# A gated sum of a recurrent attention and a feed forward part: the feed forward part goes ahead of the attention

## The chip, the cores and the metric

The kernel runs on one core of one Trainium2 chip. The time is that of the device in microseconds, the median of three runs; the profile is of one further execution. TensorE is PE, VectorE DVE, ScalarE ACT, GpSimd POOL and SyncE SP.

## What is computed

For an input x of 2048 rows and 1024 columns the output is g * a + (1 - g) * b. Here g is one number per row, b is a feed forward part with 3584 inner columns, and a is an attention that goes through 64 segments of 32 rows one after another: the first 8 of the 40 rows that a segment works on are the memory, which is the output of the segment before.

```python
        for s in range(n_seg):
            xs = x[:, s * seg_len:(s + 1) * seg_len, :].copy()
            h = jnp.concatenate([mem, xs], axis=1)
            q = jnp.einsum('btd,dhe->bhte', h, Wq)
            k = jnp.einsum('btd,dhe->bhte', h, Wk)
            v = jnp.einsum('btd,dhe->bhte', h, Wv)
            scores = jnp.einsum('bhqe,bhke->bhqk', q, k) * scale
            scores = jnp.where(mask[None, None], scores, -1000000000.0)
            p = _softmax(scores, axis=-1)
            o = jnp.einsum('bhqk,bhke->bhqe', p, v)
            o = jnp.einsum('bhte,hed->btd', o, Wo)
            mem = o[:, :M, :].copy()
            outs.append(o[:, M:, :])
...
    def _B_ref(x, w_gate, w_up, w_down):
        return _gelu(x @ w_gate) * (x @ w_up) @ w_down
    x = A_x
    g = _sigmoid((x * gate_w).sum(-1, keepdims=True))
    a = _A_ref(x, A_mem0, A_Wq, A_Wk, A_Wv, A_Wo, A_seg_len)
    b = _B_ref(x, B_w_gate, B_w_up, B_w_down)
    return g * a + (1 - g) * b
```

There are 32 heads of 128. Everything is bf16; a and b do not depend on each other.

## The kernel before

**How an operation gets its place.** There is no scheduler. `op(eng, fn, rd, wr, lane)` appends an operation to its engine's list in the order in which the program calls it, and derives its waits from the regions that it reads and writes. A DMA has a lane, and waits for the one before it in its lane. Each engine runs its list in order: a DMA on SP that waits holds up all DMAs behind it on SP.

**The weights of the attention.** Wq, Wk, Wv and Wo are 8 MB each, cut into 64 pieces of 512 KB (matrix m, half of the heads u, number i). On the chip there is room for 50 (lines 336 to 355, slots of 4 KB a partition): 36 pieces have a slot of their own, and 14 slots are shared by the two halves of a piece (`PAIRS`, line 311). Odd and even segments go through the halves in the opposite order, so each shared slot is loaded anew once a segment. Neighbouring shared slots are loaded as a group (`load_group`, line 422). A load reads the input, or a scratch in DRAM in which the group lies together, if the piece has been copied there: `keep` (line 389) writes a piece from its slot to scratch. Lines 937 and 939 call it, one or two pieces a segment, from segment 1 to segment 20, 28 pieces in all.

**The start.** Sixteen tiles of x (128 rows) are loaded to `px`, transposed on PE, copied by ACT and DVE, and written to `xq_scr` and `xr_scr` (`do_x`, line 504). POOL multiplies a tile by the gate's weights into the one buffer `gp` (line 527) and DVE sums it (line 529); `gate` (line 580) makes g out of the sums. The memory is transposed (line 494), and DVE copies it into the first segment's `hT0` (line 566) behind the DMA of line 533 that loads the rest of hT0. All 50 slots are filled in the order in which segment 0 uses them. The x tiles lie in the slots of Wo until these are loaded.

**A segment.** `proj` (line 771) projects 32 rows, 8 of memory and 24 of x (line 782 for q, k and v, lines 798 and 815 for Wo; four matmuls side by side on the columns of PE). The other 8 rows of x of each segment do not feed the memory, so their projections are made for four segments at once (`fill`, line 844, matmuls of line 852), stored to `qk_scr` and `v_scr` by POOL, and loaded back when due (`load_qk`, `load_v`). In segment 0 the fills of its own group and one of the next stand in front (`fill0`). `fold` (line 823) adds the two halves of the output in DVE, line 826 first; POOL stores them to `a_scr` (line 1012). `plan` (line 903) hangs these steps at fixed places of the walk over the weights.

**After the attention.** Line 1035 projects the outputs of the 8 other rows by Wo, for 16 segments at a time (256 matmuls), and ACT stores them to `a_scr`. Then comes the feed forward part, in four blocks `fb` of 512 rows. A block has 28 units (line 1085): 8 matmuls with w_gate and 8 with w_up make 128 inner columns; ACT and DVE make gelu and product in two and three operations. All of w_gate and w_up stays on the chip. The down projection (line 1139) goes over the block's rows in two halves; w_down comes by 1 MB through three buffers `wd` (`load_wd`), 14 loads a block. In the last block it lies whole in `wdF` (line 1120). `mix` (line 1055) takes a, which `load_a` (line 643) has loaded, and makes the output out of PSUM by two DVE operations. The gate and up weights are loaded from line 659 and lines 1047 to 1049.

Of the kernel before, what the change touches and what calls it, by code (L numbers as in the profile page):

```python
# [5 lines left out]
BF16 = mybir.dt.bfloat16  # L6
FP32 = mybir.dt.float32
# [203 lines left out]
def bass_gated_mix__memory_aug_recurrent_mem_tr__geglu_ffn__prompt_kernel(  # L211
# [34 lines left out]
    with ExitStack() as es:  # L246
# [16 lines left out]
        a_scr = nc.dram_tensor("a_scr", [NSEG, 4, SEG, 256], BF16)  # L263

# [71 lines left out]
        hosts = []  # L336
        for m in "kqvo":
            for i in range(8):
                if i in PAIRS[m]:
                    hosts.append([(m, 0, i), (m, 1, i)])  # L340
                else:
                    hosts += [[(m, 0, i)], [(m, 1, i)]]
# [46 lines left out]
        def keep(k, eng="sp"):  # L389
            t = slots[home[k]]  # L390
            op(eng, lambda e: e.dma_start(at_scr(k), t[:, :]), rd=[t.r()], wr=[("D", "w", k)], lane=f"keep{eng}")
            kept.add(k)
# [84 lines left out]
        cur[0] = slots[home["o", 0, 0]].off  # L477
        NPX = min(NT, 8)
        px = [al(f"px{i}", [128, D]) for i in range(NPX)]
        pm = al("pm", [128, D])  # L480
# [4 lines left out]
        hR1 = al("hR1", [128, KC, 32])  # L485
        dl = al("dl", [128, NT], FP32)
        assert cur[0] <= top
        memT = al("memT", [128, 64], at=oRc.off)

        mT = al("mT", [128, 16, NB])  # L490
        pw(mT, lambda e: e.memset(mT[0:NB, :, :], 0.0), True)
        pw(mT, lambda e: sel(e, mT[0:NB, :, :], ALU.is_ge, NEG, 0, [[0, 16], [1, NB]], -1))

        def tr_mem(e):
            e.transpose(PBV[5][:, 64:64 + NB], mT[0:NB, :, :].rearrange("p x i -> p (x i)"), ident[0:NB, 0:NB])
            for kc in range(KC):
                ins = e.transpose(PBV[5][:, kc * 8:(kc + 1) * 8], pm[0:8, kc * 128:(kc + 1) * 128], ident[0:8, 0:8])
            return ins
# [5 lines left out]
        def do_x(T):  # L504
            t = px[T % NPX]
            b = (XO, SS)[T % 2]
            x2 = T % 2

            def f(e):
# [8 lines left out]
            op("act", lambda e: e.activation(xq[x2][:, 0:2, :, :], pv[:, 0:2], ACTF.Copy), rd=[BK(b)], wr=[xq[x2].r(0, 512)])  # L518
            op("dve", lambda e: e.tensor_copy(xq[x2][:, 2:4, :, :], pv[:, 2:4]), rd=[BK(b)], wr=[xq[x2].r(512, 1024)])
            op("dve", lambda e: e.tensor_copy(to, PBV[b].rearrange("p (k i c) -> p k i c", k=KC, i=4)[:, :, :, NR:SEG]),  # L520
               rd=[BK(b)], wr=[to_r])
            op("act", lambda e: e.dma_start(xq_scr[T, :, :, :], xq[x2][:, :, :, :].rearrange("p i k c -> p i (k c)")),
               rd=[xq[x2].r()], wr=[("D", "xq", T)], lane=f"xw{x2}")
# [26 lines left out]
        op("sp", lambda e: e.dma_start(pm[0:8, :], mem0[:, :]), wr=[pm.r()], lane="pm")  # L550
# [4 lines left out]
        load_x(2)  # L555
        firsts = lambda m, r: [first(at_step(0, m, r, n)) for n in range(8)]
        for n in range(8):
            first(at_step(0, "k", 0, n))
            if n + 3 < NPX:
                load_x(n + 3)  # L560
        op("pe", tr_mem, rd=[pm.r(), mT.r(), ident.r()], wr=[BK(5)])
        op("dve", lambda e: e.tensor_copy(mS[:, 72:80], PBV[5][:, 64:64 + NB]), rd=[BK(5)], wr=[mS.r(72, 80)])
        op("dve", lambda e: e.tensor_copy(memT[:, :], PBV[5][:, 0:64]), rd=[BK(5)], wr=[memT.r()])
        do_x(0)
        load_h(0, "pool")
        op("dve", lambda e: e.tensor_copy(hT0[:, :, NR:32], memT[:, :].rearrange("p (k c) -> p k c", k=KC)),
           rd=[memT.r()], wr=[hT0.r()])
        for T in range(1, min(NT, 4)):
            do_x(T)
        for n in range(8):  # L570
            first(at_step(0, "q", 0, n))
            if n < 4:
                load_x(NPX + n)
        firsts("v", 0)

        def some_x(lo, hi):
            for T in range(lo, min(hi, NT)):
                do_x(T)

        def gate():  # L580
            op("act", lambda e: e.activation(gal[:, :], dl[:, :], ACTF.Exp, scale=-1.0), rd=[dl.r()], wr=[gal.r()])
            op("dve", lambda e: e.tensor_scalar(out=dl[:, :], in0=gal[:, :], scalar1=1.0, scalar2=None, op0=ALU.add),
               rd=[gal.r()], wr=[dl.r()])
            op("dve", lambda e: e.reciprocal(gal[:, :], dl[:, :]), rd=[dl.r()], wr=[gal.r()])


        cur[0] = res0
        FB = min(S, 512)
        NFB = S // FB
        TB = FB // 128  # L590
        NPS = (TB + 1) // 2
        xT = al("xT", [128, TB, 4, KC, SEG])
        WD = 4
        wd = [al(f"wd{i}", [128, WD, D]) for i in range(3)]
        CH = (2, 5, 7, 7, 7)
        assert sum(CH) == NJ
        jch = [(c, jj) for c, n in enumerate(CH) for jj in range(n)]
        wg, wu = [], []
        for c, n in enumerate(CH):
            wg.append(al(f"wg{c}", [128, KC, n * 128]))  # L600
            wu.append(al(f"wu{c}", [128, KC, n * 128]))
        GT = al("GT", [128, NJ, FB])
        assert cur[0] <= top
        free = [(low, res0), (cur[0], top)]

        def al2(name, shape, dt=BF16):
            nb = shape[1] * (4 if dt == FP32 else 2)
            for k, (lo, hi) in enumerate(free):
                if lo + nb <= hi:
                    free[k] = (lo + nb, hi)  # L610
                    return al(name, shape, dt, at=lo)
            raise AssertionError(name)
        asb = [al2(f"asb{t}", [128, D]) for t in range(4)]
        tp = [al2(f"tp{t}", [128, FB], FP32) for t in range(2)]
        s1 = al2("s1", [128, FB], FP32)
        dsb = [al2(f"dsb{t}", [128, 512], FP32) for t in range(2)]
        osb = [al2(f"osb{t}", [128, D]) for t in range(2)]

# [11 lines left out]
        NWD = NJ // WD  # L630
# [12 lines left out]
        def load_a(T):  # L643
            t = asb[T % 4]
            rd = [("D", "a", s) for s in range(4 * T, 4 * T + 4)] + [("D", "ar", T // 4, g) for g in range(4)]
            for n in range(4):
                op("sp", lambda e, n=n: e.dma_start(t[32 * n:32 * n + 32, :].rearrange("p (g c) -> p g c", g=4),
                                                     a_scr[4 * T + n].rearrange("g r c -> r g c")), rd=rd,
                   wr=[("asb", T % 4, n)] if n else [t.r()], lane=f"al{T % 4}{n}")

        oR = [al(f"oR{b}", [128, RB, 32], at=slots[home["q", 0, 2]].off + b * SB * 512) for b in range(NBK)]
        rbs = [al(f"rb{i}", [128, D], at=kT.off + 1536 - 2048 * i) for i in range(2)]
        assert a_bf.off == kT.off - 512 and rbs[0].off + 2048 <= res0
# [5 lines left out]
        early = [lambda b=b: load_oR(b) for b in range(NBK - 1)] + [lambda: load_xT(0), lambda: load_w(0), lambda: load_w(1)]  # L659


# [239 lines left out]
        STORE = [(m, i) for m in "vkq" for i in PAIRS[m]]  # L901

        def plan(s):
# [11 lines left out]
            if s == 0:  # L915
                on("k", 0, 0, lambda: some_x(4, 6))
                on("k", 0, 0, lambda: fill0("k", 0, B0, "k"))
                if NG > 1:
                    on("k", 0, 0, lambda: fill0("k", 0, B1, "o", 1, hR1))
                on("q", 0, 0, lambda: some_x(6, 8))  # L920
                on("q", 0, 0, lambda: [load_x(NPX + n) for n in range(4, 8)])
                on("q", 0, 0, lambda: (firsts("k", 1), firsts("q", 1)))
                on("q", 0, 0, lambda: fill0("q", 0, B1, "q"))
                on("v", 0, 0, lambda: some_x(8, 12))
                on("v", 0, 0, lambda: fill0("v", 0, B2, "o"))
                on("k", 0, 4, lambda: some_x(12, 16))
                on("k", 0, 4, lambda: [do_x(T) or load_x(T + NPX) for T in range(16, NT)])
                on("k", 0, 4, gate)
                on("k", 0, 5, lambda: firsts("v", 1))
                on("v", 0, 5, lambda: (firsts("o", 0), firsts("o", 1)))  # L930
# [4 lines left out]
            if 3 <= s < 3 + 2 * len(STORE):  # L935
                sm, si = STORE[(s - 3) // 2]
                on(*(("o", 1, 2) if sm == "v" else ("v", 1, 4)), lambda: keep((sm, ub, si), "act"))
            if 1 <= s <= 2 * len(PAIRS["o"]):
                on("k", 0, 4, lambda: keep(("o", s % 2, PAIRS["o"][(s - 1) // 2])))
# [86 lines left out]
        load_oR(NBK - 1)  # L1026
        for b in range(NBK):
            rb = rbs[b % 2]
            for hf in range(2):
# [9 lines left out]
                cp[("act", "dve")[hf]](rb[0:RB, hf * 512:hf * 512 + 512], PB[bk][0:RB, :], [BK(bk)], [rb.r(hf * 512, hf * 512 + 512)],  # L1039
                                       *([[ended]] if hf and b < 2 else []))  # L1040
                for g in (2 * hf, 2 * hf + 1):
                    op("act", lambda e, b=b, g=g, rb=rb: e.dma_start(a_scr[SB * b:SB * b + SB, g, NR:SEG, :], rb[0:RB, 256 * g:256 * g + 256]),
                       rd=[rb.r(256 * g, 256 * g + 256)] + [("D", "a", t) for t in range(SB * b, SB * b + SB)], wr=[("D", "ar", b, g)],
                       lane=f"sr{g}")


        load_w(2)
        load_w(3)
        load_w(4)
        for n in range(3):  # L1050
            load_wd()
# [132 lines left out]
```

## Time and profile before

| What | Value |
|---|---|
| median of 3 runs | 2289.18 us (2288.94 to 2291.22) |
| the profiled execution | 2283.55 us |
| its span, first to last instruction | 2281.7 us |
| mean granted TensorE clock | 0.982 |
| PE busy | 2054.7 us (90%) |
| DVE, ACT, POOL busy | 1044.2, 541.3, 423.7 us |
| moved by DMA | 647.47 MB, mean 284 GB/s |
| of it by queue q1 | 596.58 MB |

The busy time is an average over very different stages, so stages are read one by one. A row of the timeline is: start and length in us, engine, line, operation, what it writes and reads, how many, and in brackets the idle time before it and what ended it. The rows of DMA issues give size and the median time from issue to landing.

### The profile page before, as it was taken

The numbers are of one execution on the slowest core, as the hardware profiler recorded it, in microseconds if no ns is written. First come the engines' busy times: TensorE is split into PE (matmuls) and PEld (weight loads), VectorE is DVE, ScalarE is ACT, GpSimd is POOL, SyncE is SP. The second block draws the span as 40 slices with busy tenths as digits, with TensorE's granted clock in tenths as the row PEclk, the third lists the DMA queues.
The fourth block names the chain that finished last, engine by engine and source line by source line (L and its number), as shares of the span: only waits on it lengthen the run. The fifth ranks groups of instructions, "written<-read, shape, count | busy, mean of one in ns | idle before, by whom it ended". The sixth has DMA issues, their size and how long they took to land.

```text
span 2281.7 us, 69881 instructions
## 1 busy us (share of the span) xinstructions
PE 2054.7 (90%) x31393; PEld 979.5 (43%) x31393; DVE 1044.2 (46%) x2697; ACT 541.3 (24%) x1111; POOL 423.7 (19%) x819
## 2 busy tenths in 40 slices
PE   3498888989899999999999989998899999999999
PEld 2243444434444444444444444444454444444444
DVE  3344444444444545454554545454316346163462
ACT  1122222222222222222222222222113123031230
POOL 4422222222222222322222222221100000000000
PEclk9799999999999999999999999999999999999999
DMA  9999999989999999899999999899963530804420
GB/s 368 366 310 351 338 359 347 351 317 333 351 338 354 336 340 352 333 350 342 355 340 358 341 356 336 339 348 342 347 215 100 181 124 14 291 19 136 164 88 19
DMA packets 207002, 647.47 MB, mean 284 GB/s; under 512 B 21704, under 2 KB 90568, under 8 KB 174832
## 3 DMA queue, kind: packets, MB, share of 16 engines
q1 hardware_dynamic: 180288, 596.58, 71.8%
q0 software_dynamic: 13888, 26.31, 3.5%
q10 hardware_dynamic: 12528, 20.13, 2.4%
q8 instruction: 246, 4.03, 0.7%
q14 instruction: 52, 0.43, 0.1%
HBM read 596.85 MB, written 46.07 MB: 282 GB/s over the span
## 4 chain that ended last, share of the span: by engine, by line
PE 60%; DMA 29%; DVE 5%; ACT 2%; issue 2%; POOL 2%; SPq 0%; ACTq 0%; POOLq 0%; DVEq 0%
PE pb L782 20%; PE pb L1085 15%; DMA wall<-o_scr 10%; PE pb L1139 5%; PE pb L798 5%; DMA sl<-in_A_Wv_dram 3%; DMA o_scr<-oRc 3%; PE pb L680 3%; PE pb L1035 3%; PE pb L815 2%; PE pb L1120 2%; DMA qk_scr<-1S 2%; PE pb L852 2%; DMA wall<-in_A_Wo_dram 2%; DMA qk_scr<-0S 2%
## 5 line engine op out<-in xcount | busy, mean ns | idle before, releaser
L782 PE MATMUL pb<-sl,hT 128*32 128x512 bf16 x12288 | 765.5, 383 | 31.2 <-DMA sl<-in_A_Wv_dram 14.1
L782 PEld LDWEIGHTS pb<-sl,hT 128*32 128x32 bf16 x12288 | 306.8, 97 | 345.0 <-DVE hT L839 27.7
L852 PE MATMUL pb<-sl,hR 128*32 128x512 bf16 x3072 | 217.6, 391 | 2.1 <-issue 1.4
L1085 PE MATMUL pb<-xT,wg 128*128 128x512 bf16 x896 | 211.7, 379 | 0.7
L1085 PE MATMUL pb<-xT,wu 128*128 128x512 bf16 x896 | 211.7, 379 | 0.0
L815 PE MATMUL pb<-wall,oT 128*32 128x256 bf16 x4056 | 154.6, 280 | 34.8 <-DMA wall<-o_scr 25.4
L765 POOL COPY oRc<-oT 128x128 bf16<-128x128 bf16 x128 | 96.5, 754 | 436.6 <-DVE oT L666 436.6
L826 DVE COPY part<-pb 64x256 f32<-64x256 f32 x128 | 54.0, 422 | 261.0 <-PE pb L815 260.1
L798 PE MATMUL pb<-wall,oT 128*32 128x512 bf16 x2048 | 150.6, 392 | 5.3
L1139 PE MATMUL pb<-wd,GT 128*128 128x512 bf16 x672 | 146.0, 379 | 2.4 <-DMA wd<-in_B_w_down_dram 2.4
L1093 ACT ACTIVATE s<-pb 128x512 f32<-128x512 f32 x112 | 66.8, 596 | 312.6 <-PE pb L1085 312.6
L815 PEld LDWEIGHTS pb<-wall,oT 128*32 128x32 bf16 x4056 | 98.9, 98 | 94.9 <-DMA wall<-o_scr 28.2
L1094 DVE SCALAR_TENSOR_TENSOR tp<-s,pb 128x512 f32<-128x512 f32 x112 | 76.9, 686 | 125.0 <-ACT s L1093 124.8
L1085 PEld LDWEIGHTS pb<-xT,wg 128*128 128x128 bf16 x896 | 87.2, 98 | 107.9 <-DVE GT L1101 3.7
L1085 PEld LDWEIGHTS pb<-xT,wu 128*128 128x128 bf16 x896 | 87.7, 98 | 105.7
L666 DVE COPY kT<-pb 128x512 bf16<-128x512 bf16 x128 | 54.4, 425 | 169.4 <-PE pb L680 169.1
L716 ACT ACTIVATE E<-pb 128x320 bf16<-128x320 f32 x128 | 55.9, 437 | 311.3 <-DVE pb L715 311.3
L663 ACT ACTIVATE oS<-pb 128x512 bf16<-128x512 f32 x65 | 38.8, 597 | 373.4 <-PE pb L782 368.0
L881 POOL COPY kT<-qkr 128x128 bf16<-128x128 bf16 x128 | 37.3, 291 | 447.4 <-DVE tAB L728 219.3
L666 DVE CAST oT<-pb 128x160 bf16<-128x160 f32 x256 | 76.4, 320 | 88.0 <-PE pb L748 88.0
L728 DVE STREAM_TRANSPOSE tAB<-pAB 128x128 bf16<-128x128 bf16 x512 | 114.1, 280 | 4.4
L1098 DVE SCALAR_TENSOR_TENSOR tp<-tp,pb 128x512 f32<-128x512 f32 x112 | 77.0, 687 | 78.5 <-ACT tp L1097 78.5
(103 smaller groups left out, 2192.3 us busy)
## 6 DMA issues: line engine op xcount, KB each, us to landing
sl<-v_scr SPq DMA_DIRECT2D x55, 1536.0 KB, 10.0
wall<-o_scr SPq DMA_DIRECT2D x53, 1536.0 KB, 9.5
wall<-o_scr SPq DMA_DIRECT2D x126, 512.0 KB, 5.2
sl<-v_scr SPq DMA_DIRECT2D x51, 1024.0 KB, 9.4
sl<-k_scr SPq DMA_DIRECT2D x47, 1024.0 KB, 5.6
sl<-q_scr SPq DMA_DIRECT2D x43, 1024.0 KB, 8.1
wd<-in_B_w_down_dram SPq DMA_DIRECT2D x42, 1024.0 KB, 5.5
sl<-in_A_Wq_dram SPq DMA_DIRECT2D x21, 1024.0 KB, 9.6
```

What stands on the lines that cost most here:

```text
L666: op("dve", lambda e: e.tensor_copy(o, i), rd=rd, wr=wr, after=after)
L680: ins = e.transpose(PBV[bank][:, j * 128:(j + 1) * 128], st[:, j * 128:(j + 1) * 128], ident[:, :])
L728: return [op("dve", lambda e, c=c: e.transpose(tAB[:, c + 32 * k:c + 32 * k + 4 * w].rearrange("p (j x) -> p j x", j=4)[:, :, 0:32], pAB[: ...
L765: op("pool", lambda e: e.tensor_copy(oRc[:, :, 16 * u:16 * u + 16].rearrange("p c x -> p x c"), oT[:, :, :, 32:40].rearrange("p g j c -> p ...
L782: ins = e.matmul(PB[bk][32 * g:32 * g + 32, :], lhsT=h[:, i, :], rhs=w[:, g * 512:(g + 1) * 512], start=(n == 0), stop=(n == 7))
L798: ins = e.matmul(PB[XO][32 * g:32 * g + 32, :], lhsT=oT[:, j, x, 0:32], rhs=wall[:, na:nb + 1:nb - na, c:c + 256], start=(n == 0 and hp == 0),
L815: ins = e.matmul(PB[XO][32 * g:32 * g + 32, 256 * b:256 * b + 256], lhsT=oT[:, j, x, 0:32], rhs=w[:, c:c + 256], start=False, stop=(n % 4 ...
L852: ins = e.matmul(PB[b][32 * g:32 * g + 32, :], lhsT=h[:, k[2], :], rhs=w[:, g * 512:(g + 1) * 512], start=(n == 0), stop=(n == 7))
L1085: ins = e.matmul(PB[bk][:, 0:FB], lhsT=w[:, kc, cc:cc + 128], rhs=xT[:, :, :, kc, :].rearrange("p t i c -> p (t i) c"), start=(kc == 0), s ...
L1094: op("dve", lambda e, hg=hg, t=t: e.scalar_tensor_tensor(out=t[:, :], in0=s1[:, :], scalar=1.0, in1=hg, op0=ALU.add, op1=ALU.mult), rd=[BK ...
L1098: op("dve", lambda e, hu=hu, t=t: e.scalar_tensor_tensor(out=t[:, :], in0=t[:, :], scalar=1.0, in1=hu, op0=ALU.add, op1=ALU.mult), rd=[BK( ...
L1139: ins = e.matmul(PB[bank[2 * k + hf]][:, :], lhsT=GT[:, j, tb * 128:(tb + 1) * 128], rhs=w[:, jj, hf * 512:(hf + 1) * 512], start=(j == 0) ...
```

## The change

The feed forward part is moved in front of the attention, whole. Its buffers lie in the slots of the attention's weights, and a new order of the 50 slots (`hosts`) fits to when each of these buffers comes free. Its result is (1 - g) * b, by one DVE operation, and is stored to a scratch `b_scr`; g is stored to two scratches, in two layouts.

The first four x tiles go straight into `xT`; the other twelve are transposed between the units of blocks 0 to 2. The 28 pieces that share slots are copied from the inputs to their scratch by a DMA of their own, DRAM to DRAM, 14 in block 1 and 14 in block 2, on SP in one lane; `keep` is gone. The slots are filled on SP in block 3 (`begin`), each when its buffer is free. The last block's down projection has the same form as the others'.

Segment 0 no longer holds x tiles, the gate, or first loads. Behind the attention a, b and g are loaded, DVE makes g * a + b (`blend`) for the 24 rows of each segment, and for the other 8 straight out of PSUM behind their projection; both are stored to the output.

```diff
+        b_scr = nc.dram_tensor("b_scr", [NSEG, SEG, D], BF16)
+        g_scr = nc.dram_tensor("g_scr", [128, NT], FP32)
+        gt_scr = nc.dram_tensor("gt_scr", [NSEG, SEG, 1], FP32)
...
-        def keep(k, eng="sp"):
-            t = slots[home[k]]
-            op(eng, lambda e: e.dma_start(at_scr(k), t[:, :]), rd=[t.r()], wr=[("D", "w", k)], lane=f"keep{eng}")
+        def spread(k):
+            op("sp", lambda e: e.dma_start(dst(at_scr(k), k) if k[0] == "o" else at_scr(k), src(k)), wr=[("D", "w", k)], lane="spread")
             kept.add(k)
...
+            xo = (xT[:, T, :, :, :], lambda i, j: xT.r(1024 * T + 256 * i, 1024 * T + 256 * j)) if T < TB else (
+                xq[x2][:, :, :, :], lambda i, j: xq[x2].r(256 * i, 256 * j))
...
+        def mix(T, c0, c1, b):
+            ob = osb[T % 2]
+            op("dve", lambda e: e.tensor_scalar(out=ob[:, c0:c1], in0=PB[b][:, 0:c1 - c0], scalar1=oml[:, T:T + 1], scalar2=None, op0=ALU.mult),
+               rd=[BK(b), oml.r()], wr=[ob.r(c0, c1)])
+            op("act", lambda e: e.dma_start(b_scr[4 * T:4 * T + 4, :, c0:c1].rearrange("s r c -> (s r) c"), ob[:, c0:c1]),
+               rd=[ob.r(c0, c1)], wr=[("D", "b", T, c0)], lane=f"bo{T % 2}{c0 // 512}")
+
+        def gate(fb):
...
+            op("pool", lambda e: e.dma_start(g_scr[:, c], gal[:, c]), rd=[r(gal)], wr=[("D", "g", fb)], lane="gs")
+            for T in range(TB * fb, TB * fb + TB):
+                op("pool", lambda e, T=T: e.dma_start(gt_scr[4 * T:4 * T + 4, :, :].rearrange("s r o -> (s r) o"), gal[:, T:T + 1]),
+                   rd=[r(gal)], wr=[("D", "gt", T)], lane=f"gt{T % TB}")
...
+        load_x(2)
+        load_x(3)
+        load_w(0)
+        op("act", lambda e: e.dma_start(pmv[0:8, :], mem0[:, :]), wr=[pm.r()], lane="pm")
+        load_w(1)
+        for T in range(TB):
+            do_x(T)
+            load_x(T + NPX)
+        gate(0)
+        op("pe", tr_mem, rd=[pm.r(), mT.r(), ident.r()], wr=[BK(6)])
...
+        load_h(0, "pool")
+        op("dve", lambda e: e.tensor_copy(hT0[:, :, NR:32], memT[:, :].rearrange("p (k c) -> p k c", k=KC)),
+           rd=[memT.r()], wr=[hT0.r()])
+        load_w(2)
+        load_w(3)
+        load_w(4)
+        for n in range(3):
+            load_wd()
+        copies = [(m, u, i) for m in "ovkq" for u in (1, 0) for i in PAIRS[m]]
...
+                T = TB * (fb + 1) + (j - 3) // 6
+                if fb < NFB - 1 and j in (3, 9, 15, 21):
+                    do_x(T)
+                    load_x(T + NPX)
+                if fb < NFB - 1 and j == 25:
+                    gate(fb + 1)
+                if fb in (1, 2) and j % 2 == 1:
+                    spread(copies.pop(0))
+                if fb == NFB - 1:
+                    for n in {0: range(11), 23: range(13, 20)}.get(j, ()):
+                        begin(n)
...
+            if fb + 1 < NFB:
+                load_xT(fb + 1)
+            else:
+                for n in (11, *range(20, 29)):
+                    begin(n)
...
+                    if not end:
+                        load_wd()
+                    elif ps == NPS - 1:
+                        for n in (29 + 2 * c, 30 + 2 * c, 43 + c):
+                            begin(n)
...
+        while todo:
+            mix(*todo.pop(0))
+        begin(12)
...
+        def blend(T):
+            t, w = asb[T % NA], bsb[T % NA]
+            op("dve", lambda e: e.scalar_tensor_tensor(out=w[0:NM, :], in0=t[0:NM, :], scalar=gM[0:NM, T:T + 1], in1=w[0:NM, :],
+                                                       op0=ALU.mult, op1=ALU.add),
+               rd=[t.r(), w.r(), gM.r()], wr=[w.r()])
+            op("act", lambda e: e.dma_start(o3[4 * T:4 * T + 4, 0:NR, :], w[0:NM, :]), rd=[w.r()], wr=[("D", "out", T)], lane=f"ol{T % NA}")
...
-            if 3 <= s < 3 + 2 * len(STORE):
-                sm, si = STORE[(s - 3) // 2]
-                on(*(("o", 1, 2) if sm == "v" else ("v", 1, 4)), lambda: keep((sm, ub, si), "act"))
-            if 1 <= s <= 2 * len(PAIRS["o"]):
-                on("k", 0, 4, lambda: keep(("o", s % 2, PAIRS["o"][(s - 1) // 2])))
...
+                while mixed < NT and mixed < 2 * (2 * b + hf) + 3:
+                    blend(mixed)
+                    mixed += 1
+                    if mixed + NA - 1 < NT:
+                        load_a(mixed + NA - 1)
+                op("dve", lambda e, b=b, bk=bk, ob=ob, lo=lo, hi=hi: e.scalar_tensor_tensor(
+                    out=ob[0:RB, lo:hi], in0=PB[bk][0:RB, :], scalar=gR[0:RB, b:b + 1], in1=brb[b][0:RB, lo:hi], op0=ALU.mult, op1=ALU.add),
+                   rd=[BK(bk), gR.r(), ("gR", b), brb[b].r()], wr=[ob.r(lo, hi)])
```

## Prediction

> **What bounds the kernel now.** I read the busy digits over the span first, then the stretches of the stages, then the DMA issues and the timelines of the beginnings.
>
> ```profile
> ## 2 busy tenths in 40 slices
> PE   3498888989899999999999989998899999999999
> ...
> DMA  9999999989999999899999999899963530804420
> ```
>
> Up to slice 29 (1654 us: the attention) the DMA row is at nine tenths; behind it (the feed forward part) PE is, and the transfers are mostly idle. The first slices have full DMA and little PE.
>
> The boundaries of the stretches are times of the trace: line 826 (one pair of copies per segment) runs first at 124.19 us, for segment 22 at 682.79, for 62 at 1608.15, for 63 at 1633.89; the first feed forward matmul starts at 1693.6 and the last ends at 2278.7. The columns are length, then busy time (and instructions) of PE, weight loads, DVE, ACT, POOL, then granted clock, DMA share, GB/s.
>
> ```profile
> 0.00:124.19 124.19, 60.19 (x779) 29.27 (x783) 41.50 (x87) 20.95 (x38) 51.44 (x59) 0.82 0.98 359
> 124.19:682.79 558.60, 484.17 (x9756) 228.52 (x9744) 253.77 (x771) 134.54 (x298) 132.78 (x270) 0.98 0.95 341
> 682.79:1608.15 925.36, 848.94 (x17472) 408.47 (x17472) 459.77 (x1396) 240.26 (x534) 235.09 (x482) 0.99 0.93 345
> 1608.15:1633.89 25.74, 22.47 (x422) 11.29 (x422) 11.11 (x34) 5.20 (x12) 3.90 (x9) 0.87 0.96 359
> 1633.89:1693.76 59.87, 57.17 (x257) 37.05 (x258) 3.76 (x7) 2.39 (x4) 0.54 (x1) 0.97 0.69 215
> 1693.76:2278.70 584.94, 581.79 (x2717) 264.87 (x2714) 273.39 (x401) 137.98 (x225) 0.00 (x0) 1.00 0.37 121
> ```
>
> Segments 1 to 22 take 558.60/22 = 25.39 us each, 23 to 62 take 925.36/40 = 23.13. The rate of the transfers is the same (341 and 345 GB/s), the bytes are not: 25.39 x 341 = 8.66 MB against 7.98 MB. The 0.68 MB more, 22 times, is 15 MB: the 28 pieces of 512 KB (14.7 MB) that lines 937 and 939 write to scratch. So the early segments are bound by transfers, and the writes make them longer. The first 124 us are bound by 44.6 MB of transfers (359 x 124.19), of which 26 MB fill the 50 slots. The feed forward part is bound by PE (581.79 of 584.94) with 0.37 of the DMA in use.
>
> **The change, part by part.**
>
> *Start, 25 us.* Nothing of the attention is loaded ahead; PE's first unit (gate and up of one 128 columns, 16 matmuls, 96.69/28 = 3.45 us by the chain) needs four transposed x tiles.
>
> ```profile
> 6.12 2.12 POOL L527 TENSOR_TENSOR gp<-px,gwb 128x1024 f32<-128x1024 bf16 x1 [0.95 <-DMA px<-in_A_x_dram]
> ...
> 8.27 1.22 DVE L529 TENSOR_REDUCE dl<-gp 128x1 f32<-128x1024 f32 x1
> ...
> 14.71 0.72 POOL L533 DMA_DIRECT2D hT<-xq_scr  x1 [6.48 <-DMA xq_scr<-xq]
> ...
> 20.13 0.18 DVE L566 COPY hT<-memT 128x64 bf16<-128x64 bf16 x1 [10.64 <-DMA hT<-xq_scr]
> ```
>
> One gp buffer makes product and reduction take turns, 3.35 us a tile, and a tile's copies stand behind the reduction before: 9.5, 12.8, 16.2, and the fourth tile's copies (0.42 + 0.28) end at 16.9. Units 1 and 2 run, into four banks. DVE then still has the last reduction (19.5), the gate (20.2), and the copy into hT0, which waits for load_h on POOL; in the new order five small POOL stores stand before that load (0.55 us each by the row of v_scr, 2.18 for four; to 22.9), and it lands 5.4 us later (14.71 to 20.1 above), at 28.3. Only then come the three DVE and one ACT step of unit 1 (about 2.7 us, rows of 0.69 and 0.63): unit 3 starts near 31.3, as if the part had begun at 31.3 - 6.9 = 24.4. Queued behind the waiting copy is all DVE work of the units; PE waits for it. Bounds: 17 (no such wait) to 33 (weights 8 us late; 4.9 MB stand ahead of unit 3 and take 13.7 us at 359 GB/s). I take 25.
>
> *Feed forward, 584.9 + 7.2.* Same matmuls. Twelve x tiles are transposed inside blocks 0 to 2, on the bound engine: 8 transposes took 0.62 us warm at 63.52, so 12 x 0.6 = 7.2 us; bounds 6.5 to 12.4 (1.03 cold). Their copies (DVE 1.9 us, ACT 0.6) hide: DVE works 2.1 us of each 3.45, and bank pairs take turns. The product on POOL is ready long before. The mix falls from two DVE operations (0.69 + 0.75) to one; it was hidden, so nothing. Stores of b go out on ACT's queue with free DMA.
>
> *The 28 copies, 0.* They sit on SP in one lane, each waiting for the one before, 14 in block 1 and 14 in block 2; behind them on SP stand the xT load and the reloads of wd. No DRAM to DRAM copy is in the trace. Rows for one piece:
>
> ```profile
> wall<-o_scr SPq DMA_DIRECT2D x126, 512.0 KB, 5.2
> ...
> o_scr<-wall SPq DMA_DIRECT2D x10, 512.0 KB, 12.1
> v_scr<-sl ACTq DMA_DIRECT2D x10, 512.0 KB, 6.0
> ...
> k_scr<-sl ACTq DMA_DIRECT2D x4, 512.0 KB, 10.5
> ```
>
> All of them landed beside transfers at 0.95; the fastest that touched wall took 3.6. So one copy takes d between 3.6 and 12.1 us. Block 2's copies start when block 1 ends, and the first wd reload stands behind them, due 96.7 + 3.5 = 100 us later: no delay while 14 d is under 100, d under 7.1. In block 1 four copies come after the load of x at unit 22 (about 76 us): d under 6. I take 5.5, near the fast rows because DMA is otherwise idle there: nothing. Beyond it each block loses about 14 d - 100. The Trainium skill (DMA: Bandwidth & Descriptors, section Latency and other measured facts) gives 207 GB/s for copies between HBM tensors at one large row pitch; by it, an estimate, a piece moves in 2.5 us and d stays under the threshold. No run here shows it yet.
>
> *Loads of the slots, 0 in block 3.* Eleven pieces go at its first unit, seven at unit 24, ten behind the units, 21 in the last 24.2 us of down projections, one behind the last mix. The 21 are 11 MB, 32 us at 345 GB/s: they end some 8 us into segment 0, which uses the first of them about 20 us in. wdF is loaded as before.
>
> *Segment 0, 64 us up to its first fold (line 826 now).* PE needs the fills of group 0, one of group 1, and serial round trips by scratch. I build it from rows: mix of bank 5 1.2; fill 1.9, ACT 0.6, transposes 0.4, DVE 0.42, to the first qk_scr store at 5; three stores in one lane, each 5 to 6.4 us (rows of 100.00 and 106.96), to 21.4; qkr loaded at 27.6 (6.2, median); scores, softmax and vB (4.8) to 34.
>
> ```profile
> 93.94 0.24 PE L748 MATMUL pb<-tAB,vB 32*128 32x64 bf16 x4 [0.57 <-DMA vB<-v_scr]
> ...
> 94.78 3.35 PE L852 MATMUL pb<-sl,hR 128*32 128x512 bf16 x32 [0.60 <-ACT oT L663]
> ...
> 100.70 1.90 PE L852 MATMUL pb<-sl,hR 128*32 128x512 bf16 x32
> ```
>
> From 94.78 on the order is the old one: 124.19 - 94.78 = 29.4. Together 63.7. Bounds 52 (quick round trips, 3.6 each) to 75 (weights 10 us late). The first of these fills took 3.35 us and the later one 1.90, since PE had been idle before it. The Trainium skill (TensorE: Matmul & The Clock Gate, section Why this matters for your kernels) speaks against such gaps: after about 3 us of idle PE runs at half rate. By it, the gap before unit 3 would cost 1.5 to 1.7 us more, within the bounds of the start; the pair 3.35 and 1.90 agrees.
>
> *Segments 1 to 62.* No copying beside them, all shared pieces from scratch from the first on: 62 x 23.13 = 1434.3. Segment 63: 25.74.
>
> *End, 59.87 + 3.0.* The 256 matmuls of the last projection bound it as before (54 us behind the first 6). DVE gets 16 blends of 96x1024 and 8 of 128x512; by the 0.75 us of the present 128x512 a blend is at most 1.5, so 30 of 54 us: hidden. The last operation and its store of 128 KB replace one of 64 KB; before took 3.0.
>
> **Sum**: 25 + 584.9 + 7.2 + 64 + 1434.3 + 25.7 + 59.9 + 3.0 = 2204 us, against a span of 2281.7: minus 78. The profiled execution took 2283.55, 1.85 over its span; the median shown, 2289.18, is 5.63 above it. Forecast for the median: 2204 + 1.85 + 5.63 = 2211 us.
>
> **Rivals.**
> - *Copies hold up SP* (slower). In block 1 and 2 the wd reload comes late by 14 d - 100. At d = 10 both blocks lose 40 us and the gain of 78 is gone; from there on the kernel is slower. At 12.1 (the row of o_scr, on this same queue): 2 x 69 = 139, 2350 us. For it: that row, and ten of the copies read 1 KB rows of Wo. Against: it queued behind loads on a DMA at 0.95, where block 1 and 2 leave it idle. Chance 0.10; a lesser lag, d of 7 to 9.5, 2211 to 2280: 0.08.
> - *Early segments stay slow*: if their 2.26 us come from something that stays, 22 x 2.26 = 50 us return: 2261. Against: the bytes account for 15 MB / 345 GB/s = 43 of the 50. The place of the scratch in DRAM shifts, too; one per cent of rate is 14 us either way. Chance 0.12.
>
> **How the numbers follow.** Forecast 0.70, its own range 2190 to 2235 (start -8 to +8, x tiles to +5, segment 0 -12 to +11, steady pace half a per cent). With the lesser lag and the second rival in part, 2188 to 2255; what is left out is the slower rival and the tails. About 0.2% (4.6 us) is what a measurement here tells from no change. Faster 0.88, same 0.02, slower 0.10.
>
> **What would show it.** The chain's DMA wd wait in blocks 1 and 2 near 7.6 us as now, and copies landing in under 6; the folds 23.1 us a segment apart from the second segment on, the first one about 64 us behind the last down projection; PE idle some 6 us between the second and third unit; no wd rise. The forecast is wrong if SP's copies land at 8 us or more, if the early segments keep 25 us, or if weights arrive more than 30 us into segment 0.

## The result and the profile after

The changed kernel takes 2299.39 us (median of 5 runs, 2296.93 to 2304.75), the kernel before in the same session 2289.02 (median of 5, 2286.58 to 2291.22): a ratio of 1.005, 95% interval 1.0032 to 1.0068. It is slower by 0.5%, where 2211 us had been forecast. The profiled execution took 2304.75 us with a span of 2302.9; the forecast's sum for the span was 2204, so 99 us have to be found.

First the busy tenths of the changed kernel.

```profile
span 2302.9 us, 69850 instructions
...
## 2 busy tenths in 40 slices
PE   5999989999968999899999999999999989998880
...
DMA  9255385293577899899999898999999989998932
```

Each slice is 57.6 us. The order is turned: the feed forward part (PE at nine, DMA at two to eight) ends in slice 12, the attention with full DMA follows. Two things stand out against the page of before: a busy DMA row of only 3 and 2 in the last two slices while PE falls to 8 and 0, and single slices of DMA 9 in the feed forward part.

The stretches of the changed kernel (length, then busy time of PE, weight loads, DVE, ACT, POOL, granted clock, DMA share, GB/s). The first two are the down projections of blocks 0 and 3; then segment 0 up to its first fold, segments 1 to 22, 23 to 62, 63, and what follows the last segment.

```profile
133.80:189.40 55.60, 51.31 (x225) 22.33 (x224) 4.10 (x6) 0.46 (x1) 0.28 (x1) 0.94 0.84 265
...
600.00:648.50 48.50, 48.50 (x225) 21.80 (x223) 4.10 (x6) 0.44 (x1) 0.00 (x0) 1.00 0.77 276
648.50:709.53 61.03, 38.97 (x642) 16.91 (x646) 14.36 (x39) 10.02 (x20) 13.71 (x25) 0.83 0.60 217
709.53:1223.20 513.67, 477.18 (x9756) 229.22 (x9744) 253.89 (x771) 134.71 (x298) 132.89 (x270) 0.99 0.92 342
1223.20:2153.40 930.20, 851.16 (x17472) 408.43 (x17472) 459.79 (x1396) 240.68 (x534) 234.99 (x482) 0.99 0.92 343
2153.40:2179.31 25.91, 22.70 (x422) 11.23 (x422) 11.12 (x35) 5.20 (x12) 3.62 (x8) 0.84 0.96 357
2179.31:2302.90 123.59, 56.80 (x256) 36.87 (x256) 27.55 (x28) 0.00 (x0) 0.54 (x1) 0.73 0.39 122
```

| Stage | forecast, us | profile, us | difference |
|---|---|---|---|
| start and feed forward part, to its last matmul | 617.1 | 648.5 | +31 |
| segment 0, to its first fold | 64 | 61.0 | -3 |
| segments 1 to 62 | 1434.3 | 1443.9 (23.29 each) | +10 |
| segment 63 | 25.7 | 25.9 | 0 |
| end | 62.9 | 123.6 | +61 |

The early segments did become short: 513.67/22 = 23.35 us each, 25.39 before. That gain of 45 us is there. It is given back at the two ends.

**The end.** PE has 56.8 us of work in a stretch of 123.6. The stretch cut in three, the last part after PE's last matmul at 2238.5:

```profile
2179.31:2190.00 10.69, 8.28 (x32) 4.80 (x33) 1.68 (x4) 0.00 (x0) 0.54 (x1) 0.76 0.93 254
2190.00:2240.00 50.00, 48.53 (x225) 32.07 (x223) 9.55 (x9) 0.00 (x0) 0.00 (x0) 1.00 0.39 121
2240.00:2300.00 60.00, 0.00 (x0) 0.00 (x0) 16.32 (x16) 0.00 (x0) 0.00 (x0) 0.52 0.30 101
```

PE works undisturbed in the second row and has nothing in the third. But the DMA share is only 0.39 and 0.30, at 121 and 101 GB/s, though SP has loads to issue all the time. The answer for the tile of a (duration of an issue: least, median, most; then the instructions that use the tile) and the heads of the chain of waits in this window say what it is:

```profile
L780 SPq DMA_DIRECT2D asb<-a_scr x64: 607/898/3541, 2188.1 to 2286.9; - x64
L789 DVE SCALAR_TENSOR_TENSOR bsb<-asb,gM,bsb x16: 1279/1280/1281, 2197.1 to 2296.5; 96x1024 bf16<-96x1024 bf16 x16
its engine sat idle before it (us, times) until:
  DMA bsb<-b_scr: 91.5, 16
```

```profile
by line: SPq L780 58.7%; SPq L782 15.1%; DMA bsb<-b_scr 6.9%; SPq L752 3.7%; issue 3.7%; SPq L774 2.9%; SPq L767 2.2%; SPq L770 2.0%; DVEq L1174 1.5%; SPq L143 0.1%; DVE bsb L789 0.0%
```

DVE needs 16 x 1.28 us for the blends and waits 91.5 us for loads. SP's issues of a and b (lines 780 and 782) are the chain. A share of 0.30 is about 4.8 of the 16 transfer engines. Counted packet by packet in the trace, four or five packets are in flight for 36 of the 40 us from 2245 to 2285. In DRAM these loads have the form of 4 segments x 24 rows x columns (`a_scr[4 * T:4 * T + 4, n, 0:NR, :]`), and so have the stores of the output. This form is new: the kernel before loads a by one DMA of 32 rows per segment. The packets of these three groups, added up over the stretch and divided by 4, are 43 us for a, 40 for b and 33 for the output, together 116.

**The start.** DVE's timeline (start, length, engine, line, operation; in brackets the idle time before and what ended it):

```profile
20.17 0.18 DVE L661 COPY memT<-pb 128x64 bf16<-128x64 bf16 x1
37.25 0.18 DVE L663 COPY hT<-memT 128x64 bf16<-128x64 bf16 x1 [16.89 <-DMA hT<-xq_scr]
37.34 0.68 DVE L689 SCALAR_TENSOR_TENSOR tp<-s,pb 128x512 f32<-128x512 f32 x1
```

The copy into hT0 is where it was expected in the order, and all of DVE's unit work does stand behind it; but it waits until 37.25 and not until 28.3. Unit 3 starts at 40.18. The loads of the whole execution (size, median us from issue to landing):

```profile
wd<-in_B_w_down_dram SPq DMA_DIRECT2D x42, 1024.0 KB, 6.3
...
xT<-xq_scr SPq DMA_DIRECT2D x3, 1024.0 KB, 12.0
...
k_scr<-in_A_Wk_dram SPq DMA_DIRECT2D x4, 512.0 KB, 4.9
q_scr<-in_A_Wq_dram SPq DMA_DIRECT2D x4, 512.0 KB, 4.3
...
gt_scr<-gal POOLq DMA_DIRECT2D x16, 0.5 KB, 9.1
...
hT<-xq_scr POOLq DMA_DIRECT2D x1, 64.0 KB, 13.9
```

Before, the load of hT0 landed in 5.4 us, xT in 5.6, wd in 5.5. The stores of one column of g to `gt_scr`, 512 bytes each, take 9.1 us, longer than a copy of 512 KB. And what moves behind them in the first gap, at the end of block 0 (128 to 150 us in 40 slices; 134 is where the xT load begins):

```profile
DMA  0000000000000620064494013299999999999999
GB/s 0 0 0 0 4 1 1 1 1 0 0 0 7 160 52 19 7 30 7 11 30 7 4 7 34 63 186 346 413 406 406 413 410 384 391 380 395 380 395 372
```

The xT load is issued and for 7 us almost nothing moves; then all of it at 400 GB/s. The down projections behind take 55.6, 58.2 and 55.2 us in blocks 0 to 2, and 48.5 in block 3, which has no gate in front. In the kernel before, those of blocks 0 to 2 take 49.2 to 49.4. Against 49.2 they are 6.4 + 9.0 + 6.0 = 21 us longer; with the 8.9 us at unit 3 that is 30 of the 31.

**What did not happen.** The 28 copies did not hold up SP. Their time to landing (least, median, most):

```profile
DMA to landing us min/median/max: 3.6/4.2/6.8
```

The median is under the 6 and 7.1 us that the forecast allowed in blocks 1 and 2 before SP would be late; only the longest copy in block 1, at 6.8, is over.

### The profile page after: what moved, and what is told of

Read it like the earlier page. It is cut to its first block, busy times and chain, and to the rows that moved or that the text cites. A ratio compares the mean times of both kernels' runs of the same rounds, so it can differ in the third digit from the quotient of the medians.

```text
span 2302.9 us, 69850 instructions
## 1 busy us (share of the span) xinstructions
PE 2051.2 (89%) x31365; PEld 975.8 (42%) x31365; DVE 1042.1 (45%) x2689; ACT 539.0 (23%) x1110; POOL 434.2 (19%) x839
## 4 chain that ended last, share of the span: by engine, by line
PE 62%; DMA 21%; DVE 6%; SPq 5%; ACT 3%; issue 2%; POOL 1%; ACTq 0%; DVEq 0%; POOLq 0%
PE pb L916 24%; PE pb L680 13%; DMA wall<-o_scr 10%; PE pb L732 7%; PE pb L932 5%; PE pb L814 3%; SPq L780 3%; PE pb L949 3%; DMA o_scr<-oRc 3%; PE pb L986 2%; DMA wd<-in_B_w_down_dram 2%; DMA sl<-v_scr 1%; DVE oT L800 1%; PE pb L874 1%; DMA qk_scr<-1S 1%
## 5 line engine op out<-in xcount | busy, mean ns | idle before, releaser
L986 PE MATMUL pb<-sl,hR 128*32 128x512 bf16 x3072 | 212.9, 385 | 3.2 <-DVE osb L621 1.5
L732 PE MATMUL pb<-wd,GT 128*128 128x512 bf16 x672 | 154.1, 393 | 15.4 <-DMA wd<-in_B_w_down_dram 15.4
L732 PEld LDWEIGHTS pb<-wd,GT 128*128 128x128 bf16 x672 | 67.1, 101 | 102.0 <-DMA wd<-in_B_w_down_dram 18.6
```

The costliest lines, as they stand in the source:

```text
L732: ins = e.matmul(PB[bank[2 * k + hf]][:, :], lhsT=GT[:, j, tb * 128:(tb + 1) * 128], rhs=w[:, x, hf * 512:(hf + 1) * 512], start=(j == 0), ...
L986: ins = e.matmul(PB[b][32 * g:32 * g + 32, :], lhsT=h[:, k[2], :], rhs=w[:, g * 512:(g + 1) * 512], start=(n == 0), stop=(n == 7))
```

## The experiments

Two theories. A, for the end: loads and stores whose DRAM side has 4 as its outermost size (4 segments) are carried by only 4 transfer engines; its rivals are the number of loads on SP, and that blends or stores bound it. B, for the start: the 4-byte stores to neighbouring places of `gt_scr` stop the memory for several us at each gate, and with it the loads behind; its rivals are the number of DMAs on POOL's queue, the packing of these stores into packets, and the copies. In the table the pace is taken between the first copies of folds 0 and 62, and the end runs from the first copy of fold 63; these columns are of one profiled execution each, and each ratio is against the kernel before in the same session.

| Kernel | median, us | ratio to before (95%) | last feed forward matmul begins | segments 1 to 62, each | end |
|---|---|---|---|---|---|
| changed | 2299.39 | 1.0032 to 1.0068 | 648.1 | 23.29 | 123.6 |
| e1 loads and stores of the end by segment | 2241.13 | 0.968 to 0.990 | 646.2 | 23.31 | 66.9 |
| e2 only the stores | 2281.23 | 0.994 to 1.000 | 646.1 | 23.25 | 105.4 |
| e8 only the loads of a | 2275.99 | 0.994 to 0.997 | 642.7 | 23.26 | 101.0 |
| e3 no 4-byte stores | 2264.77 | 0.981 to 0.998 | 614.8 | 23.17 | 121.4 |
| e4 4-byte stores 512 bytes apart | 2275.93 | 0.991 to 0.997 | 616.7 | 23.35 | 124.6 |
| e9 64 bytes apart | 2267.38 | 0.985 to 0.995 | 618.2 | 23.15 | 124.5 |
| e10 4-byte stores twice | 2335.28 | 1.014 to 1.025 | 677.1 | 23.36 | 123.8 |
| e7 copies undone | 2347.17 | 1.024 to 1.029 | 640.3 | 23.96 | 124.5 |
| e5 = e1 and e3 | 2206.35 | 0.964 to 0.967 | 611.6 | 23.20 | 66.6 |
| e6 = e5, hT0 later | 2206.33 | 0.964 to 0.967 | 609.2 | 23.28 | 64.3 |

**e1, the end by segment.** a is loaded by one DMA per segment, 32 rows of 128, b by one of 128 rows, and the output is stored by four DMAs of 24 rows (the 8 rows more per segment are loaded and not stored).

```diff
-   op("sp", lambda e, n=n: e.dma_start(t[0:NM, 256 * n:256 * n + 256], a_scr[4 * T:4 * T + 4, n, 0:NR, :]),
+   op("sp", lambda e, n=n: e.dma_start(t[32 * n:32 * n + 32, :].rearrange("p (g c) -> p g c", g=4), a_scr[4 * T + n].rearrange("g r c -> r g c")),
...
-   op("sp", lambda e: e.dma_start(w[0:NM, :], b_scr[4 * T:4 * T + 4, 0:NR, :]),
+   op("sp", lambda e: e.dma_start(w[:, :], b_scr[4 * T:4 * T + 4].rearrange("s r c -> (s r) c")),
...
-   op("act", lambda e: e.dma_start(o3[4 * T:4 * T + 4, 0:NR, :], w[0:NM, :]),
+   for n in range(4):
+       op("act", lambda e, n=n: e.dma_start(o3[4 * T + n, 0:NR, :], w[32 * n:32 * n + NR, :]),
```

> Only the end differs from the changed kernel: a and b are loaded as tiles of 128 rows (a by segment, 32 rows a DMA; b as one block of 128 rows), the blend runs over 128 rows, and its 24 rows of each segment are stored by one DMA per segment. Theory A: the loads and stores of the changed kernel have a DRAM side whose slowest dimension is 4, so only 4 of the 16 DMA engines carry them; 9.4 MB at the 98 GB/s seen there are 96 us. Then the stretch from the last fold to the end falls from 123.6 us to 64 to 70, bound by PE again, and the run gets 54 to 60 us faster (about 2240). Rival B: SP takes 0.6 us and more to issue each of its 5 DMAs per tile, whatever their shape; there are still 5 per tile, so the stretch stays over 105 us.

The end takes 66.9 us. Its stretch from 2190 to 2240, and the issue of the same 64 loads:

```profile
2190.00:2240.00 50.00, 49.23 (x225) 32.70 (x228) 24.07 (x23) 0.00 (x0) 0.00 (x0) 1.00 1.02 281
```

```profile
L780 SPq DMA_DIRECT2D asb<-a_scr x64: 375/432/2336, 2189.2 to 2234.7; - x64
```

The DMA share goes from 0.39 to 1.02 with more bytes to move (the share adds up packets, so it can pass 1), and 15 or more packets are in flight for 38 of the 40 us from 2195 to 2235. An issue on SP takes half as long, 432 ns against 898. Not all of this is waiting for the few engines: the least is 607 ns in the changed kernel and 375 here, so the form itself has a price, and the waits lie above it. The Trainium skill (DMA: Bandwidth & Descriptors, section Why a DMA increments its semaphore by 16 and not by 1) states the rule: a DMA is spread over the largest number of engines up to 16 that divides the outermost size, other than 1, of both sides; 4 segments against 96 partitions give 4, and here 32 against 32 for a and 128 against 128 for b give 16. The packets in flight, four or five before and 15 or more now, agree with it.

**e2 and e8, one group each.** e2 splits only the stores of the output (the last part of the diff above, with 24 rows a segment in the buffer as well); e8 loads only a by segment, in 24 rows.

> Only the stores of the blended rows differ from the changed kernel: one DMA of 24 rows per segment instead of one of 96 rows per tile, on ACT. SP's DMAs are as in the changed kernel. Theory A: 6.3 MB instead of 9.4 are left on 4 engines, 64 us at 98 GB/s, so the end falls by about 32 us, from 123.6 to some 92. Rival B (SP's issues set the pace): SP's list is the same, the end stays at 120 to 124 us.

> Of the last stage only the loads of a are changed, to one load per segment of 24 rows in place of one per 256 columns; their number and their bytes stay. If the time of the end is the summed work of the four busiest transfer engines (a 43 + b 40 + out 33 us by the packets, 116 of the 123.6), and the new loads of a go over 12 engines, the four have 14 + 40 + 33 = 87 and the end takes 90 to 99 us. If instead the number of loads on SP sets it (64 + 16 issues, unchanged), the end stays at 119 to 125. If only the loads' latency in turn mattered, it would fall to the 67 of the first experiment, since a's are four of five loads.

The ends take 105.4 and 101.0 us. Each group takes its part off the end, and neither alone is the cause: 64 + 16 loads stay in both, so their number is not it. But both gains are smaller than expected (some 92, and 90 to 99). If the new transfers go over 12 engines that include the 4, the sums are 43 + 40 + 11 = 94 and 14 + 40 + 33 = 87; both ends are 11 to 14 us above that (the changed kernel's 8 above 116). The sum of packets thus has the direction right and is 6 to 14% too small. Part of it in e2 is that its stores' packets take 197 us in all and not the 133 of the changed kernel, 16 us over 12 engines in place of 11; what the rest is was not tried.

**e3, e4, e9, e10, the small stores.** e3 leaves `gt_scr` out; the column that the last mixing needs is read from `g_scr` by 16 small loads in block 2. e4 and e9 keep the stores and put each 4 bytes in a place of its own, 512 and 64 bytes apart (the diff is e4's; e9 has 16 in place of 128). e10 stores each column a second time, into another tensor that nothing reads.

```diff
-        gt_scr = nc.dram_tensor("gt_scr", [NSEG, SEG, 1], FP32)
+        gt_scr = nc.dram_tensor("gt_scr", [NSEG, SEG, 128], FP32)
...
-   op("pool", lambda e, T=T: e.dma_start(gt_scr[4 * T:4 * T + 4, :, :].rearrange("s r o -> (s r) o"), gal[:, T:T + 1]),
+   op("pool", lambda e, T=T: e.dma_start(gt_scr[4 * T:4 * T + 4, :, 0:1].rearrange("s r o -> (s r) o"), gal[:, T:T + 1], ...),
```

> The second scratch of g, written as 16 stores of 128 single elements of 4 bytes (four per block), is left out; the column that the end needs is read once, in block 3, from the first scratch of g. The end is otherwise as in the changed kernel. Theory C: the 4-byte stores hold up the memory for about 10 us each time, and the loads behind them: xT lands in 12 us, hT0 in 13.9. Without them xT lands in 5.5 us, the down projections of blocks 0 to 2 take 49 to 50 us instead of 55.2 to 58.2, unit 3 starts some 8 us earlier, and the last feed forward matmul ends near 618 to 622 us instead of 648.5: 26 to 30 us faster. Rival D: xT is slow because xq_scr was written shortly before, or by the stores of b: nothing changes, 648.

> The 16 stores of 4-byte elements stay, but each element goes to a line of its own 512 bytes from the next one, instead of 128 elements side by side in 512 bytes. If it is the stores into the same few lines that hold up the memory, xT lands in 5.5 to 7 us and the feed forward part ends near 622. If it is the mere number of small stores, xT stays at 12 us and the feed forward part ends at 645 to 652. By rival D nothing changes either.

> The 4-byte stores of g each go to a place of their own 64 bytes apart, in place of 4 (changed kernel) or 512 bytes (fourth experiment). If only stores whose 64 bytes are shared hold each other up, this is as good as the 512: a store of one column lands in 1.7 us (9.1 in the changed kernel), unit 3 starts at 29 to 32 and the feed forward part ends at 613 to 618. If a wider piece of the memory is what is shared (eight of these stores lie in each 512 bytes), a part of the delay stays: landing at 3 to 8 us, an end of the feed forward part at 622 to 645. If the cause was the packing of eight stores in one packet, the packets tell: it is the same in all three.

> The dose: at each gate the four columns are stored twice, the second time into a further tensor of the same shape (its content is not read). If each 4-byte store into a shared line costs a time of its own, one after the other, the loads behind a gate are held up twice as long: about 10 us more at each of the four gates, and the feed forward part ends at 675 to 692 in place of 643 to 650; the kernel takes 30 to 42 us more than the changed one. If the two tensors' lines are worked on side by side, or the stall has a fixed length, the end moves by less than 12 us.

Without the stores the last feed forward matmul begins at 614.8 us, some us earlier than expected, with unit 3 at 29.5 and the down projections at 48 to 50. With as many stores, by the same queue, of the same bytes, each in its own place, it is nearly the same: 616.7 and 618.2, with unit 3 at 31.5 and 32.0. So POOL's queue and the number of stores account for 2 to 3 of the 31 us, and neighbourhood for the rest. Packing does not differ: in the changed kernel, e4 and e9 alike, each of the four columns of a gate goes out in 16 packets of 32 bytes. The DMA rows of e9:

```profile
xT<-xq_scr SPq DMA_DIRECT2D x3, 1024.0 KB, 5.5
...
gt_scr<-gal POOLq DMA_DIRECT2D x16, 0.5 KB, 1.7
...
hT<-xq_scr POOLq DMA_DIRECT2D x1, 64.0 KB, 5.7
```

and of e10:

```profile
xT<-xq_scr SPq DMA_DIRECT2D x3, 1024.0 KB, 20.8
...
gt_scr<-gal POOLq DMA_DIRECT2D x16, 0.5 KB, 9.5
gt_two<-gal POOLq DMA_DIRECT2D x16, 0.5 KB, 16.7
hT<-xq_scr POOLq DMA_DIRECT2D x1, 64.0 KB, 19.2
```

A column lands in 1.7 us when each store has 64 bytes to itself, in 9.1 when 16 share them. The delay grows about in proportion to the stores: the xT load behind takes 5.5 us with none, 12.0 with 512 shared stores ahead of it, 20.8 with 1024, which is 13 to 15 ns a store; the feed forward part ends some 30 us later (e4 and e9 to the changed kernel) and then another 29 (to e10). This looks as if the stores were worked off one after the other, and loads of other addresses wait meanwhile. Why those wait is not shown. The Trainium skill (DMA: Bandwidth & Descriptors, section Back-pressure in remote DMA) says, of writes between cores, that a stalled write also stalls the other queues of its transfer engine; that fits what is seen here with DRAM, and no run tells it from a stall in the memory.

**e7, the copies undone.** The copies beside the feed forward part are left out: `keep` and its two lines in `plan` are back, `spread` is out.

```diff
-                if fb in (1, 2) and j % 2 == 1:
-                    spread(copies.pop(0))
...
+            if 3 <= s < 3 + 2 * len(STORE):
+                sm, si = STORE[(s - 3) // 2]
+                on(*(("o", 1, 2) if sm == "v" else ("v", 1, 4)), lambda: keep((sm, 1 - s % 2, si), "act"))
+            if 1 <= s <= 2 * len(PAIRS["o"]):
+                on("k", 0, 4, lambda: keep(("o", s % 2, PAIRS["o"][(s - 1) // 2])))
```

> One part of the change is undone alone: the 28 copies beside the feed forward part are left out, and the pieces are written to scratch from their slots during segments 1 to 20 by the lines of the kernel before. If those writes made the early segments slow (14.7 MB at 345 GB/s = 43 us), folds 0 to 22 now come 25.2 to 25.5 us apart instead of 23.35, folds 22 to 62 stay at 23.1 to 23.3, the feed forward part still ends at 645 to 650, and the kernel takes 40 to 48 us more than the changed one: 2336 to 2348 us. If the early segments were slow for another reason that the change removed along with the writes, they stay at 23.4 and the kernel takes 2295 to 2305. If the copies had slowed the feed forward part, it now ends before 640.

Segments 1 to 22 and 23 to 62 of this kernel:

```profile
701.60:1259.30 557.70, 482.99 (x9756) 226.20 (x9744) 253.49 (x771) 134.55 (x298) 133.03 (x270) 0.99 0.96 341
1259.30:2187.30 928.00, 851.71 (x17472) 407.93 (x17472) 459.44 (x1396) 240.37 (x534) 235.18 (x482) 0.99 0.93 345
```

25.35 us each, as in the kernel before, and 23.20: the writes made the early segments slow, and 48 us in the median come back with them (2347.17 against 2299.39, of two sessions). The copies were the gain. Its feed forward part ends at 640.3, 8 us earlier than the changed kernel's; this lies between the expectation for copies that cost nothing (645 to 650) and for copies that do (before 640). By blocks, 2 of the 8 us lie in block 0, ahead of the first copy; the units of blocks 1 and 2 take 99.6 us each against 99.7 and 100.8, and the down projections behind them 55.5 and 53.7 against 58.2 and 55.2. So at most 5 to 6 us are the copies'; e8, with the copies, ended at 642.7.

**e5 and e6, both causes away.**

```diff
-        load_h(0, "pool")
-        op("dve", lambda e: e.tensor_copy(hT0[:, :, NR:32], ...
...
+                if fb == 0 and j == 5:
+                    load_h(0, "pool")
+                if fb == 0 and j == 7:
+                    op("dve", lambda e: e.tensor_copy(hT0[:, :, NR:32], ...
```

> Both suspected costs taken away at once: the loads of the last stage go in 128-row pieces (as in the first experiment) and the 4-byte stores of g are left out (as in the third). If the two causes are separate, their gains add: the feed forward part's last matmul ends at 615 us (as in the third), the first fold comes 61 us later (676), the segments take 23.2 to 23.3 us each, and from fold 63 to the end it is 67 us (as in the first): a span of 2200 to 2210 and a median of 2202 to 2214 us, a ratio of 0.963 to 0.970, which is the forecast's 2211. If the two shared a cause (one slow memory for both), the second gain is smaller: above 2220 us, with an end above 80 or a feed forward part that ends after 630.

> The same, and in addition the load of hT0 and the copy into hT0 behind it are recorded five and seven units later, so that VectorE's work of units 1 to 3 no longer stands behind the copy that waits for that load. If that wait alone kept unit 3 until 29.5 us (third experiment), unit 3 now starts at 21 to 25, right behind the gate's operations, and everything after it comes 5 to 8 us earlier than in the kernel without this edit: the feed forward part ends at 607 to 611 and the median is 5 to 8 us lower. If instead the weights of the units (4.9 MB ahead of unit 3) hold it, unit 3 stays at 28 to 30 and the two kernels take the same time.

e5 takes 2206.35 us, 3.5% less than before (ratio 0.9652, 0.9639 to 0.9666), the fastest kernel here together with e6. Its stages lie near those that had been forecast:

```profile
611.80:671.90 60.10, 39.20 (x644) 16.80 (x646) 14.33 (x38) 10.01 (x20) 13.77 (x25) 0.83 0.61 223
671.90:1185.40 513.50, 473.49 (x9756) 228.02 (x9748) 253.65 (x771) 134.80 (x298) 132.80 (x270) 0.99 0.92 342
1185.40:2110.20 924.80, 847.53 (x17472) 407.78 (x17472) 459.49 (x1397) 240.36 (x534) 235.49 (x482) 0.99 0.93 346
2110.20:2136.00 25.80, 21.73 (x422) 10.47 (x422) 11.09 (x35) 5.20 (x12) 3.62 (x9) 0.87 0.97 358
2136.00:2202.60 66.60, 57.95 (x256) 36.95 (x256) 27.60 (x28) 0.00 (x0) 0.54 (x1) 0.94 1.00 259
```

Its span of 2202.6 us is close to the 2204 of the forecast's sum, but in part by luck: start, feed forward part and segment 0 are 9 us shorter than forecast, segments 1 to 62 and the end 8 us longer. The two gains add: 2299.39 - 58 (e1) - 35 (e3) = 2206; with two runs each of e1 and e3, 14 and 6 us apart, the agreement to the microsecond is chance. In e6 unit 3 starts at 25.43 instead of 29.51, so the wait for hT0 did hold it; the feed forward part ends 2.4 us earlier where 5 to 8 had been expected, and the median is the same. Its first fold even comes later, at 673.1 against 671.9, so segment 0 gives the gain back; why is open.

## Why the prediction was wrong

- **End, 59.87 + 3.0: the step that failed most, by 61 us.** "DVE gets 16 blends ... 30 of 54 us: hidden" is right about DVE: its work is 27.6 us. But only the engine's work was priced. The loads of a and b and the stores of the output, which the change puts into this stretch, were given no time at all. Their packets need 116 us on the few engines that they get. e1 changes their form alone (and loads 8 rows more per segment), and 57 of the 61 us are gone.
- **Start, 25 us, and feed forward, 584.9 + 7.2: 31 us too small**, by one mis-sized term. The "five small POOL stores" were priced at 0.55 us of issue each, and the load behind them at the 5.4 us of the old trace. What they cost is not on POOL: each set of four columns holds up the loads behind it by 6 to 9 us, four times, and the first time DVE's whole queue stands behind the load. With the stores harmless (e3) unit 3 starts at 29.5 where 31.3 had been worked out, and the part ends at 615 where the sum has 617.1: the rest of this step was right. Of it the x tiles cost a little more than taken: the units of blocks 1 and 2 of e5 take 99.6 and 100.5 us against 96.7 in block 3 (in e7, without copies, 99.6 both), which is 2.9 and 3.8 a block where 2.4 had been taken, within its bounds.
- **The 28 copies, 0: right, to within the 5 to 6 us that e7 leaves open.** They land in 4.2 us in the median where 5.5 was taken and 7.1 allowed, so the rival that ended on the slower side, copies that hold up SP, did not happen. The kernel is slower all the same, by two mechanisms that were not among the rivals. The Trainium skill's rate for such copies (DMA: Bandwidth & Descriptors, section Latency and other measured facts), 2.5 us a piece by the estimate, agrees in that nearly all stay under the threshold; the shortest here took 3.6 in all.
- **Segment 0, 64 us: right** (61.0, in e5 60.1). Its two parts, 34 and 29.4, make 63.4 and not 63.7; nothing hangs on it.
- **Segments 1 to 62, 62 x 23.13: the mechanism right** (e7), the early segments at 23.35. The pace came out 0.16 us higher, 10 us in all: 0.7%, more than the half per cent that the narrower range allowed for. Over the ten kernels with copies it lies between 23.15 and 23.36 and follows none of the edits; what sets it stays open.
- **The range**, 2188 to 2255, was built of bounds on the priced steps. What was missing were the prices of two groups of small or oddly cut transfers, and no bound covers a term that is not in the sum.

## What to carry over

When a change moves work to where it seems to be hidden, price the transfers that it brings with it as well as the engine's operations, by the form that they have in DRAM: the outermost size decides how many transfer engines carry them. Do not scatter single values to neighbouring addresses while anything else is to be loaded; in this kernel it was enough to give each its own 64 bytes. A change whose mechanism is right can end slower: look at the stages one by one before it is given up, since here two small repairs bring 2299 us to 2206.

## What the runs showed of the hardware

- 512 stores of 4 bytes into neighbouring places take 9.1 us a column to land, and a 1 MB load from elsewhere behind them lands 6.5 us later (12.0 against 5.5); behind twice as many it lands 15.3 us later (20.8). With the stores 64 bytes apart they land in 1.7 us and the load in 5.5.
- When only few transfer engines take the loads, it shows on the issuing queue: an issue on SP took 898 ns in the median (607 to 3541) where the same number of loads over all engines took 432 (375 to 2336). With only the stores respread (e2) it took 679.
- A copy of 512 KB from DRAM to DRAM, on a DMA with room, lands in 4.2 us in the median, less than the median of any group of loads of that size in the changed kernel (5.1 is the lowest, of 131 loads beside the attention's transfers).
